# Attention and MLP on one core: quads of four heads on four 64x64 tiles of the array, for batches 2 to 7

## The chip, the cores and the metric

The kernel runs on one core of a Trainium2 chip. The core has a matrix engine (TensorE, PE in the profile; its weight loads are listed apart as PEld), VectorE (DVE), ScalarE (ACT), GpSimd (POOL), which also issues one kind of DMA, and SyncE (SP), which issues the other kind. The engines run their own instruction streams, each in its written order, and wait for one another through semaphores. PE multiplies a stationary operand (loaded into the array as weights, up to 128 rows by 128 columns) with a moving one that streams through, and writes to PSUM: 8 banks, each 128 partitions of 512 fp32 numbers. DVE and ACT read PSUM and write to SBUF. A matmul can use a part of the array: 64 of its rows (a row tile), 64 of its columns (a column tile) or both (64x64). The metric is the device time of a run in microseconds, lower is better.

## The reference

```python
def _attn_ref(q, k, v):                       # (8, 12, 448, 64) each
    scale = 1.0 / np.sqrt(q.shape[-1])
    scores = scale * np.matmul(q, k.transpose(0, 1, 3, 2))
    m = np.max(scores, axis=-1, keepdims=True)
    e = np.exp(scores - m)
    attn = e / (np.sum(e, axis=-1, keepdims=True) + np.exp(-m) + 1e-09)
    return np.matmul(attn, v)

x = attn_out.transpose(0, 2, 1, 3).reshape(B * S, H * D)   # 3584 x 768
h = x @ w_in                                               # 768 x 2048
r = np.maximum(h, 0.0)
out = (r * r) @ w_out                                      # 2048 x 768
```

The softmax has a one added to its denominator. The kernel uses exp(scores) without the maximum, so the denominator is the sum plus 1. Inputs and outputs are fp32, the kernel's operands fp16.

## The kernel before

Attention is worked in units of a batch and a pair of heads; x is kept transposed (`xts`, features on partitions). For one unit the 448 keys are cut into four chunks of 112 (key 4p+t is row p of chunk t). `scores` makes, per chunk, the transposed scores of both heads in PSUM (112 keys on partitions, 2 x 448 queries), and one ACT instruction turns them into exponentials (`exp`, 112x896) in a buffer `et`. In batches 0 to 2 (`ON_PE`) q and k are transposed by PE; there, each head holds 64 partitions. From batch 3 on, a DMA transposes them from a staged fp16 copy in DRAM, which lays even and odd tokens on the two halves of the partitions; so a chunk takes four matmuls of 224 queries, two of them in flight as row tiles of 64 rows. `values` accumulates V times exponentials over the four chunks, the two heads as column tiles (112 rows, 64 columns). `add_chunks` sums the four chunks on DVE; `row_sums` multiplies that by ones (two matmuls), and ACT takes Ln(x + 1) and Exp(-x), the reciprocal `rcp`; `normalise` multiplies values and reciprocal on DVE into `xts`.

The MLP: `tile_in` is a tile of the first product: 128 hidden features by 448 tokens, 6 steps of 2 column tiles (128 rows, 64 columns), then relu and square on DVE (`relu_squared`, two instructions) into a ring `gs`. `tile_out` is a half-tile of the second product: 128 tokens by 384 columns, 16 steps. In the mode `ROWS2` a step is two row tiles (64 rows, 128 columns), which write two banks, `op` and `lo`; DVE reads `op` (L359) and then adds `lo` to it (L363). A batch has 16 tiles of the first product and on the mean 7 half-tiles of the second.

The order of the work is written out by hand (`manual_schedule`). From batch 2 on, the loop takes three units at a time. It goes over their 12 score chunks, and between two chunks it runs 4 or 5 steps of `tile_out` in `ROWS2` (`rows`). Then, in the mode `COLS2`, come the values of the three units before (`take_in`), then `tile_in` tiles with sums between them (`sum_up`). The first product of batch b-1 and the second of b-2 run beside the attention of batch b. After the first three units of a batch, the transposing loads of batch b+1 go to SP's queue; on POOL, `hold` waits for them with a tiny copy, and behind it stand V of b+1 and the staged copy of b+2.

PSUM: scores have two buffers of two banks. Everything else takes one-bank buffers from `mp_tile`, in turn three of `m_psum` and one of `x_psum`: a tile gets its bank once the tile that had it before has been read, and PE waits for that at the new tile's first matmul. A half-tile in `ROWS2` takes two of the four.

Of the kernel before, what the change touches and what calls it, by code (L numbers as in the profile page):

```python
# [8 lines left out]
FP32 = mybir.dt.float32  # L9
# [6 lines left out]
def kernel(  # L16
# [16 lines left out]
    NFFB = DF // 128  # L33
    RUN = 4
    P = S // RUN
    ON_PE = (0, 1, 2)
    COLS = H * S // 2 + 16
    HALF = DM // 2
# [34 lines left out]
    wout_r = moe_w_out.rearrange("(c p) f -> p c f", p=128)  # L73

    whole, vns, qks, xts, naturals, stages = {}, {}, {}, {}, {}, {}

    def load_v(b, p0, p1):
        hs = slice(2 * p0, 2 * p1)
# [62 lines left out]
            )  # L141


    def cast(b, pr):
        for name in "qk":
            f = flat.tile([P, 2, RUN, D], FP16, name=f"flat{name}")
            if pr < 2 and name == "k":
                nc.scalar.activation(out=f, in_=naturals[name, b, pr], func=AF.Copy)
            else:
                nc.vector.tensor_copy(f, naturals[name, b, pr])  # L150
            naturals[name, b, pr] = f
# [26 lines left out]
    def scores(u, et, c, only=(0, 1)):  # L178
        b, pr, q0, n = u
        qk = qks[b]  # L180
        two = [] if n == S else s_psum.tile([P, 2, 512], FP32, name="sp")
        for kk in [2 * c + x for x in only]:
            sp = s_psum.tile([P, 2, 512], FP32, name="sp") if n == S else two
            if b in ON_PE:
                o = 0 if n == S else kk % 2 * n
                for h in range(2):
                    r = slice(64 * h, 64 * h + 64)
                    x = pr * S
                    nc.tensor.matmul(sp[:, h, o:o + n], qk[r, 1, x + P * kk:x + P * kk + P],  # L189
                                     qk[r, 0, x + q0:x + q0 + n], start=True, stop=True)  # L190
            else:
                for h in range(2):
                    for odd in range(2):
                        r = slice(64 * odd, 64 * odd + 64)
                        x = (2 * pr + h) * (S // 2)
                        kx = x + kk // 2
                        which = 1
                        if kk % 2 != odd:
                            which = 2
                            kx += kk % 2  # L200
                        nc.tensor.matmul(sp[:, odd, h * (S // 2):(h + 1) * (S // 2)],  # L201
                                         qk[r, which, kx:kx + 2 * P - 1:2], qk[r, 0, x:x + S // 2],
                                         start=True, stop=True)
            if n == S:
                exp(chunk(et, u, c, kk).rearrange("p (o x) -> p o x", o=2), sp[:, :, 0:S])
        if n < S:
            exp(et[:, 0:RUN * 2 * n].rearrange("p (c h x) -> p c h x", c=2, h=2)[:, c], two[:, :, 0:2 * n])
# [15 lines left out]
    def of_head(e, u, h):  # L223

        b, _, _, n = u
        if n < S:
            return e[:, h]
        if b in ON_PE:
            return e.rearrange("p (h x) -> p h x", h=2)[:, h]
        return e.rearrange("p (o h x) -> p h o x", o=2, h=2)[:, h]  # L230

    def values(u, et, xp, o=0):
        b, pr, _, n = u
# [5 lines left out]
    def row_sums(us, sums):  # L239
# [4 lines left out]
        for j, (u, parts) in enumerate(zip(us, sums)):  # L244
            for x, es in enumerate(parts):
                total = es[:, 0:2 * n]
                if n < S:
                    total = total.rearrange("p (h n) -> p h n", h=2)
                for h in range(2):
                    nc.tensor.matmul(zp[64 * h:64 * h + 64, j * n:(j + 1) * n], ones, of_head(total, u, h),  # L250
                                     start=(x == 0), stop=(x == len(parts) - 1))
        rcp = z_pool.tile([128, 512], FP32, name="rcp")
        nc.scalar.activation(out=rcp[:, 0:m], in_=zp[:, 0:m], func=AF.Ln, bias=one_b)  # L253
# [11 lines left out]
            nc.vector.tensor_mul(xts[b][:, pr:pr + 2, q0:q0 + n], *two)  # L265


    joined = [-1]

    def mp_tile(dtype=FP32):  # L270
# [4 lines left out]

    FULL, COLS2, ROWS2 = range(3)
    mode = [FULL]
    ots = {}  # L280

# [46 lines left out]
    def store(c, ot, n0, n1):  # L328
        end = c + 128
        while c < end:  # L330
            b = c // S
            step = RUN if b in ON_PE else 2
            rows = out[b * S:(b + 1) * S, n0:n1].rearrange("(p t) m -> t p m", t=step)
            t, p = c % S // (S // step), c % S % (S // step)
            m = min(S // step - p, end - c)
            o = c + 128 - end
            nc.sync.dma_start(out=rows[t, p:p + m, :], in_=ot[o:o + m, n0:n1])
            c += m

    def tile_out(tok, n0, w):  # L340
# [1 line left out]
        if n0 == 0:  # L342
            ots[tok] = osb_pool.tile([128, DM], FP32, name="ot")
        ot = ots[tok]
        rows = mode[0] == ROWS2
        op = mp_tile()
        lo = mp_tile() if rows else None
        for fb in range(NFFB):
            g = gs[:, fb, tok % RING:tok % RING + 128]
            if rows:  # L350
                for x, o in ((0, op), (64, lo)):
                    nc.tensor.matmul(o[:, 0:w], g[x:x + 64], wout[x:x + 64, fb, n0:n0 + w],  # L352
                                     start=(fb == 0), stop=(fb == NFFB - 1))
            else:
                product(op[:, 0:w], g, wout[:, fb, n0:n0 + w], start=(fb == 0), stop=(fb == NFFB - 1))
            if fb < NFFB - 1:
# [13 lines left out]

    warm = consts.tile([128, 512], FP16)
    nc.vector.memset(warm, 0.0)
    ones = consts.tile([P, 64], FP16)
    nc.vector.memset(ones, 1.0 / GS)
    one_b = consts.tile([128, 1], FP32)
    nc.vector.memset(one_b, 1.0 / GS)
    for pr in range(3):
# [60 lines left out]

    FIRST = 192
    units = [(0, pr, 0, FIRST) for pr in range(NPAIR)] + [(0, pr, FIRST, S - FIRST) for pr in range(NPAIR)]  # L440
    units += [(b, pr, 0, S) for b in range(1, B) for pr in range(NPAIR)]
    NU = len(units)

    transpose_at = {pr - 1: [(0, pr)] for pr in range(1, NPAIR)}
    for i, at in ((10, (1, 0)), (11, (1, 1)), (11, (1, 2)), (13, (1, 3)), (14, (1, 4)), (15, (1, 5)), (16, (2, 0)),
                  (17, (2, 1))):
        transpose_at.setdefault(i, []).append(at)

    def keep_warm(n):
# [5 lines left out]
    ets, ess, rcps = {}, {}, {}  # L455
    xp = None

    last_of = consts.tile([1, 3, 1], FP16)

    def hold(b):  # L460

        nc.gpsimd.tensor_copy(last_of, qks[b][0:1, :, 0:1])

    def begin(i):
        spare = (i - 3 * NPAIR - 3) % 6
        if i > 3 * NPAIR + 2 and spare in (1, 2):
            ets[i] = nat.tile([P, RUN * 2 * S], FP16, name=f"nn{spare - 1}")
        else:
            ets[i] = e_pool.tile([P, RUN * 2 * S], FP16, name="et")
        es = es_pool.tile([P, 2 * S], FP16, name=f"es{i % 2}")  # L470
        half = es_pool.tile([P, 1024], FP16, name="half")
        ess[i] = (es, half)
# [50 lines left out]
    for i in range(NPAIR, 2 * NPAIR):  # L523
# [28 lines left out]
        if i > NPAIR:  # L552
            drain(share[0] * (0.25 if two else 0.2))
        if i == NPAIR + 5:
            load_natural(2, 0, 3)
            for n0 in (0, HALF):
                for j in range(2):
                    load_wout(n0, j, 2)
# [2 lines left out]
    for i in range(2 * NPAIR, 3 * NPAIR):  # L561
# [6 lines left out]
        scores(u, et, 0)  # L568
        for at in transpose_at.get(i, ()):
            transposes(*at)  # L570
        if i == 2 * NPAIR + 3:
            load_natural(2, 3, 6)
            load_v(2, 0, 6)
            stage(3)
        drain(share[0] * (1.2 if first else 0.45))
        scores(u, et, 1)
# [23 lines left out]

    pending = [3 * NPAIR - 1]
    joined[0] = 0
    complete(S)

    def rows(n):
        mode[0] = ROWS2
        while outs and n > 0:
            one(outs)  # L610
            n -= 1
        mode[0] = COLS2

    def take_in(at):
        xp = mp_tile()
        values(units[at], ets.pop(at), xp)
        normalise([units[at]], xp, rcps.pop(at))

    def add(at, *steps):
        for step in steps:  # L620
            add_chunks(units[at], ets[at], *ess[at], step)

    def sum_up(*ats):
        for at in ats:
            rcps[at] = row_sums([units[at]], (ess.pop(at)[0:1],))

    for i in range(3 * NPAIR, NU, 3):
        b, pr = units[i][0:2]
        for j in range(3):
            begin(i + j)  # L630
            for kk in range(RUN):
                scores(units[i + j], ets[i + j], kk // 2, (kk % 2,))
                if kk == 0 and j:
                    add(i + j - 1, 1, 2)
                if kk == 1:
                    add(i + j, 0)
                if (i, j, kk) == (3 * NPAIR, 0, 2):
                    transposes(2, 2)
                if (j, kk) != (2, RUN - 1):
                    rows(5 if (RUN * j + kk) % 3 == 0 else 4)  # L640
        mode[0] = COLS2
        if i == 3 * NPAIR:
            sum_up(i - 1)
        for at in pending:
            take_in(at)
        if b in ON_PE and pr == 0:
            for x in range(3):
                transposes(b, 3 + x)
        if pr == 0:
            queue((b - 1) * S, S)  # L650
            if b > 2:
                run(outs)
            if b + 1 < B:
                transposed_loads(b + 1)
                hold(b + 1)
                load_v(b + 1, 0, NPAIR)
                if b + 2 < B:
                    stage(b + 2)

        run(ins, 1 if pr == 0 else 2)  # L660
        add(i + 2, 1)
        run(ins, 1)
        add(i + 2, 2)
        sum_up(i, i + 1)
        run(ins, 2)
        sum_up(i + 2)
        run(ins, 3 if pr == 0 else 4)
        if pr:
            complete(b * S)
        pending = [i, i + 1, i + 2]  # L670
    for at in pending:
        take_in(at)
    mode[0] = FULL
    run(outs, 3)
    queue((B - 1) * S, S)
# [31 lines left out]
```

## Time and profile before

| | |
|---|---|
| median of 3 runs | 412.71 us (412.4 to 412.81) |
| span of the profiled execution, its own time | 410.6 us |
| PE busy | 401.9 us (98%) |
| DVE busy | 289.7 us (71%) |
| ACT busy | 234.8 us (57%) |
| POOL busy | 36.1 us (9%) |
| two batches of the steady part, 146 to 239 us | 93.0 us |

The page shows one profiled execution; its 410.6 us lie between the first and the last instruction, the runs' times also hold what lies around that. Matmuls are pipelined: one of 448 columns shows about 0.35 us while the next pair starts 0.19 us later, so the rate is read from the starts, and a busy PE is not PE at its peak. A row of instructions in order of time gives the start, how long they last together, engine, line, operation, out<-in, sizes and count; behind it, in brackets, the engine's idle time before it and who ended that. A row of waits names who waited for whom, the total in us, how often and the longest. A row of busy times has, for a stretch, its length, busy us (and instructions) of PE, PEld, DVE, ACT and POOL, PE's granted clock, the share of the DMA engines and GB/s.

### The profile page before, as it was taken

The page shows a single profiled execution, that of the slowest core. Times are in us where ns is not written, and L with a number is a line of the kernel's source. Part 1 is how long each engine was busy: PE and PEld are TensorE (multiplying, and loading weights), DVE is VectorE, ACT ScalarE, POOL GpSimd, SP SyncE. Part 2 cuts the span into 40 slices and gives each one's busy share as a digit, 9 for nine tenths or more (in the row PEclk, how much of TensorE's full clock was granted, in tenths as well). Part 3 has the DMA queues.
Part 4 walks back from the last instruction along what each step waited for, and adds up shares of the span by engine and source line. Part 5 has one row for each costly group of instructions (what it writes and reads, how often), then busy time and mean ns, then how long its engine had stood idle before and what let it go on. Part 6 is the DMA issues. An engine that isn't in the chain of part 4 may idle for free.

```text
span 410.6 us, 10684 instructions
## 1 busy us (share of the span) xinstructions
PE 401.9 (98%) x4715; PEld 261.0 (64%) x4715; DVE 289.7 (71%) x554; ACT 234.8 (57%) x312; POOL 36.1 (9%) x58
## 2 busy tenths in 40 slices
PE   8899999999999999999999999999999999999997
PEld 3577676865576666666566666667566665555664
DVE  3778889878976787777876788867876789186000
ACT  5899897767393745559383755739464663100111
POOL 7524030020000100001000030001000000000000
PEclk9999999999999999999999999999999999999999
DMA  9999999779114991499304892297102010010222
GB/s 204 197 199 196 203 202 218 134 136 215 54 42 106 137 201 42 96 186 181 102 2 115 167 179 65 78 185 127 41 2 69 11 41 2 38 40 0 78 77 78
DMA packets 75823, 45.58 MB, mean 111 GB/s; under 512 B 42560, under 2 KB 72000, under 8 KB 75456
## 3 DMA queue, kind: packets, MB, share of 16 engines
q0 software_dynamic: 28848, 22.16, 35.6%
q1 hardware_dynamic: 46208, 22.05, 23.7%
q8 instruction: 37, 0.61, 0.6%
q10 hardware_dynamic: 720, 0.69, 0.5%
q14 instruction: 10, 0.08, 0.1%
HBM read 45.69 MB, written 17.93 MB: 155 GB/s over the span
## 4 chain that ended last, share of the span: by engine, by line
PE 91%; DVE 4%; ACT 3%; issue 1%
PE mp L286 26%; PE mp L352 16%; PE mp L288 10%; PE xp L352 7%; PE xp L286 6%; PE sp L201 6%; PE mp L236 5%; PE xp L288 4%; PE xp L236 3%; PE sp L189 3%; ACT et L169 3%; PE mp L250 2%; PE mp L158 1%; PE mp L452 1%; DVE half L218 1%
## 5 line engine op out<-in xcount | busy, mean ns | idle before, releaser
L169 ACT ACTIVATE et<-sp 112x896 f16<-112x896 f32 (+2 forms) x144 | 125.6, 916 | 42.4 <-PE sp L201 30.6
L286 PE MATMUL mp<-xt,win 128*64 128x448 f16 (+2 forms) x1296 | 115.4, 325 | 0.7 <-DVE xt L262 0.6
L352 PE MATMUL mp<-wout,gs 64*128 64x384 f16 x848 | 115.1, 323 | 0.0
L286 PEld LDWEIGHTS <-win 128*64 128x64 f16 x1536 | 85.1, 110 | 44.7 <-issue 1.8
L293 DVE TENSOR_SCALAR rt<-mp 128x448 f16<-128x448 f32 (+2 forms) x104 | 64.7, 622 | 31.1 <-PE mp L286 18.5
L352 PEld LDWEIGHTS <-gs 64*128 64x128 f16 x1152 | 58.0, 94 | 21.3 <-issue 0.2
L352 PE MATMUL xp<-wout,gs 64*128 64x384 f16 x304 | 62.4, 323 | 0.0
L295 DVE TENSOR_TENSOR gs<-rt 128x448 f16<-128x448 f16 (+2 forms) x128 | 50.2, 392 | 4.4
L201 PE MATMUL sp<-qk 64*112 64x224 f16 x480 | 43.1, 258 | 0.0
L169 ACT ACTIVATE nn<-sp 112x896 f16<-112x896 f32 x48 | 41.7, 917 | 1.6
L253 ACT ACTIVATE rcp<-mp,one_b 128x448 f32<-128x448 f32 (+2 forms) x35 | 22.1, 633 | 32.2 <-PE mp L250 32.2
L361 ACT ACTIVATE ot<-mp 128x384 f32<-128x384 f32 (+2 forms) x16 | 7.5, 471 | 57.5 <-PE mp L288 41.2
L201 PEld LDWEIGHTS <-qk 64*112 64x112 f16 x480 | 30.6, 128 | 14.3 <-issue 3.6
L288 PEld LDWEIGHTS <-gs 128*128 128x128 f16 x256 | 24.4, 98 | 15.1 <-issue 0.4
L236 PEld LDWEIGHTS <-vn 112*64 112x64 f16 x432 | 22.5, 109 | 15.1 <-issue 3.2
L288 PE MATMUL mp<-wout,gs 128*128 128x384 f16 (+2 forms) x192 | 29.5, 313 | 0.0
L214 DVE TENSOR_TENSOR es<-et 112x896 f16<-112x896 f16 x30 | 18.7, 623 | 14.0 <-ACT et L169 13.6
L254 ACT ACTIVATE rcp<-rcp 128x448 f32<-128x448 f32 (+2 forms) x48 | 27.7, 577 | 1.5
L189 PE MATMUL sp<-qk 64*112 64x448 f16 (+2 forms) x192 | 26.1, 320 | 1.0 <-ACT et L169 0.4
L216 DVE TENSOR_TENSOR es<-es,half 112x896 f16<-112x896 f16 x42 | 26.2, 623 | 1.0
L286 PE MATMUL xp<-xt,win 128*64 128x448 f16 x240 | 26.1, 352 | 0.0
L262 DVE TENSOR_TENSOR xt<-mp,rcp 128x448 f16<-128x448 f32 x29 | 18.0, 621 | 2.9 <-ACT rcp L254 1.1
(63 smaller groups left out, 345.2 us busy)
## 6 DMA issues: line engine op xcount, KB each, us to landing
vn<-in_v_dram POOLq DMA_DIRECT2D x7, 672.0 KB, 8.8
out_dram<-ot SPq DMA_DIRECT2D x9, 384.0 KB, 2.3
win<-in_moe_w_in_dram POOLq DMA_DIRECT2D x8, 384.0 KB, 14.2
wout<-in_moe_w_out_dram POOLq DMA_DIRECT2D x4, 768.0 KB, 18.0
stage_q<-in_q_dram POOLq DMA_DIRECT2D x4, 676.0 KB, 11.6
stage_k<-in_k_dram POOLq DMA_DIRECT2D x4, 676.0 KB, 14.9
out_dram<-ot SPq DMA_DIRECT2D x8, 288.0 KB, 8.7
out_dram<-ot SPq DMA_DIRECT2D x9, 192.0 KB, 2.7
```

The source lines that it names most:

```text
L169: nc.scalar.activation(out=out_, in_=in_, func=AF.Exp, scale=scale)
L189: nc.tensor.matmul(sp[:, h, o:o + n], qk[r, 1, x + P * kk:x + P * kk + P], qk[r, 0, x + q0:x + q0 + n], start=True, stop=True)
L201: nc.tensor.matmul(sp[:, odd, h * (S // 2):(h + 1) * (S // 2)], qk[r, which, kx:kx + 2 * P - 1:2], qk[r, 0, x:x + S // 2], start=True, sto ...
L216: nc.vector.tensor_add(es, es, half[:, 0:2 * S])
L236: nc.tensor.matmul(xp[64 * h:64 * h + 64, o:o + n], vns[b][:, 2 * pr + h, kk, :], of_head(chunk(et, u, kk // 2, kk), u, h), start=(kk == 0 ...
L253: nc.scalar.activation(out=rcp[:, 0:m], in_=zp[:, 0:m], func=AF.Ln, bias=one_b)
L254: nc.scalar.activation(out=rcp[:, 0:m], in_=rcp[:, 0:m], func=AF.Exp, scale=-1.0)
L286: nc.tensor.matmul(out_[x:x + 64], lhsT[:, x:x + 64], rhs, start=start, stop=stop)
L288: nc.tensor.matmul(out_, lhsT, rhs, start=start, stop=stop)
L293: nc.vector.tensor_scalar(out=rt[:, 0:m], in0=hp[:, 0:m], scalar1=0.0, scalar2=None, op0=ALU.max)
L295: nc.vector.tensor_mul(gs[:, f0:f0 + per, t0 % RING:t0 % RING + n], r, r)
L352: nc.tensor.matmul(o[:, 0:w], g[x:x + 64], wout[x:x + 64, fb, n0:n0 + w], start=(fb == 0), stop=(fb == NFFB - 1))
```

## The change

In batches 2 to 7 a unit is now a quad: two pairs of heads, 4g to 4g+3 or, from batch 3 on, two of each half of the heads. The keys are cut into 7 chunks of 64. Each step on PE is four matmuls of 64 rows and 64 columns, on the four quarters of the array:

- `visit`: the scores of one chunk of a quad (64 keys of two heads on the two halves of the partitions, 2 x 448 queries), and one exponential of 128x896.
- `values_quad`: V times exponentials; row half i and column half j are the four heads; the results take two banks.
- `add_quad`: the 7 chunks summed on DVE: 1792 wide (two chunks with two), 1792, 896 and 896.
- `sums_quad`: the sums of four heads in two banks; for a batch's third quad as column tiles with `half_ones`. Ln and Exp twice on ACT, 448 wide each.
- `tile_out`: the mode `ROWS2` becomes `SQUARE`: each step's two matmuls are cut into two by columns.

A batch has three quads m, m+1, m+2. The new loop has two groups per batch, made by `between`: 11 visits with three half-tiles of the second product, then 10 visits with four. Between two visits `between` runs pieces of values or sums that are named by visit number, and steps of `tile_out` up to a share of time. Behind each group come 8 tiles of the first product, in `COLS2`. On POOL `tail_keys` (four copies of 64x384 that gather the last 64 keys) takes the place of `hold`; V comes in two or four loads a batch, q and k of batch 2 in loads of 64 partitions; batch 2's output rows are stored with a step of 7. Batches 0 and 1 and the last stage stay as they were.

```diff
+    QUADS = [(b, g) for b in range(2, B) for g in range(NQ)]
+    def visit(m, c):
+        b, g = QUADS[m]
...
+        sp = s_psum.tile([128, 2, 512], FP32, name="sp")
...
+                        h = H // 2 * i + 2 * g + j
+                        if c == KC - 1:
+                            keys = kms[b][r, h, :]
...
+                            keys = qk[r, which, x:x + 190:3]
+                        nc.tensor.matmul(sp[64 * i:64 * i + 64, o, j * n:(j + 1) * n], keys,
+                                         qk[r, 0, h * n:(h + 1) * n], start=True, stop=True)
+        exp(chunk_quad(m, c).rearrange("p (o x) -> p o x", o=2), sp[:, :, 0:S])
...
+    def sums_quad(m, in_cols):
+        es = esq.pop(m)[:, 0:2 * S]
+        zqs[m] = []
+        for i in range(2):
+            zp = mp_tile()
...
+                    r = slice(64 * i, 64 * i + 64)
+                    nc.tensor.matmul(zp[64 * j:64 * j + 64, 0:S], ones[r], of_column(es[r], m, j),
+                                     start=True, stop=True)
+            zqs[m].append(zp)
+        for i in range(2):
+            rcp = z_pool.tile([128, 512], FP32, name="rcp")
+            nc.scalar.activation(out=rcp[:, 0:S], in_=zqs[m][i][:, 0:S], func=AF.Ln, bias=one_b)
+            nc.scalar.activation(out=rcp[:, 0:S], in_=rcp[:, 0:S], func=AF.Exp, scale=-1.0)
+            zqs[m][i] = rcp
+    def values_quad(m):
+        b, g = QUADS[m]
+        xps = [mp_tile(), mp_tile()]
+        for c in range(KC):
+            e = chunk_quad(m, c)
+            for i in range(2):
+                for j in range(2):
+                    r = slice(64 * i, 64 * i + 64)
+                    nc.tensor.matmul(xps[i][64 * j:64 * j + 64, 0:S], vns[b][r, g, j, c, :], of_column(e[r], m, j),
+                                     start=(c == 0), stop=(c == KC - 1))
+            if c == KC - 1:
...
+                for i in range(2):
+                    nc.vector.tensor_mul(xts[b][:, NQ * i + g, :], xps[i][:, 0:S], zqs[m][i][:, 0:S])
...
+            yield
@@ tile_out @@
-                for x, o in ((0, op), (64, lo)):
-                    nc.tensor.matmul(o[:, 0:w], g[x:x + 64], wout[x:x + 64, fb, n0:n0 + w],
-                                     start=(fb == 0), stop=(fb == NFFB - 1))
+                for y in (0, 64):
+                    for x, o in ((0, op), (64, lo)):
+                        nc.tensor.matmul(o[y:y + 64, 0:w], g[x:x + 64, y:y + 64], wout[x:x + 64, fb, n0:n0 + w],
+                                         start=(fb == 0), stop=(fb == NFFB - 1))
@@ the loop @@
+    STEP = HALF / 2.4
+    PIECE = S / 2.4
+    def second(ns):
+        mode[0] = SQUARE
+        while outs and ns > STEP / 2:
+            ns -= one(outs)
+        return ns
+    def between(visits, tiles, ns, extras):
+        tiles = min(tiles, len(outs))
+        kept = outs[tiles:]
+        del outs[tiles:]
+        ns += tiles * NFFB * STEP
+        spent = 0.0
+        late = []
+        for n, (m, c) in enumerate(visits):
+            visit(m, c)
+            for at in late:
+                add_quad(*at)
+            late = {3: [(m, 0)], 5: [(m, 1), (m, 2)], 6: [(m, 3)]}.get(c, [])
+            spent += PIECE
+            for f in extras.get(n, ()):
+                spent += f() or 0.0
+            spent += max(0.0, (n + 1) * ns / len(visits) - spent) - second((n + 1) * ns / len(visits) - spent)
+        second(1e9)
+        outs[:] = kept
+        return late
...
+    for b in range(2, B):
+        m = NQ * (b - 2)
+        extras = {10: [summed(m)]}
+        ns = 12 * PIECE
+        if b > 2:
+            gen = values_quad(m - 1)
+            for n, w in ((1, 3), (2, 4)):
+                extras[n] = [pieces(gen, w)]
+            ns += KC * PIECE
+        between([(m, c) for c in range(KC)] + [(m + 1, c) for c in range(4)], 3, ns, extras)
         mode[0] = COLS2
...
+        queue((b - 1) * S, S)
+        if b + 1 < B:
+            transposed_loads(b + 1)
+            tail_keys(b + 1)
+            load_v_quads(b + 1)
+            if b + 2 < B:
+                stage(b + 2)
+        run(ins, 2)
+        add_quad(m + 1, 0)
+        run(ins, 6)
+        gen, gen1 = values_quad(m), values_quad(m + 1)
+        extras = {6: [summed(m + 1)]}
+        for n, w in ((0, 3), (1, 4)):
+            extras[n] = [pieces(gen, w)]
+        extras[8] = [pieces(gen1, 3)]
+        extras[9] = [pieces(gen1, 4)]
+        between([(m + 1, c) for c in range(4, KC)] + [(m + 2, c) for c in range(KC)],
+                4, (11 + 2 * KC) * PIECE, extras)
         mode[0] = COLS2
...
+        run(ins, 1)
+        add_quad(m + 2, 3)
+        run(ins, 1)
+        sums_quad(m + 2, True)
+        run(ins, 6)
+        complete(b * S)
```

## The prediction

> **What bounds the kernel now.** I read the page first, then busy times over two batches of the steady part (146 to 239 us), then PE's waits, then the instructions in order of time.
>
> ```profile
> span 410.6 us, 10684 instructions
> PE 401.9 (98%) x4715; PEld 261.0 (64%) x4715; DVE 289.7 (71%) x554; ACT 234.8 (57%) x312; POOL 36.1 (9%) x58
> PEclk9999999999999999999999999999999999999999
> 146.00:192.50 46.50, 46.50 (x568) 30.19 (x566) 35.73 (x68) 27.83 (x37) 2.14 (x4) 1.00 0.74 137
> 192.50:239.00 46.50, 46.50 (x566) 30.00 (x564) 35.73 (x68) 27.89 (x37) 3.29 (x7) 1.00 0.48 104
> PE mp L286 <- DVE xt L262: 0.6, 1, 0.6
> ```
>
> PE has work in flight all the time, at full clock, and a batch takes 46.5 us. A busy PE alone proves little, so I add the batch up from starts of instructions:
>
> ```profile
> 179.50 2.44 PE L286 MATMUL mp<-xt,win 128*64 128x448 f16 x24
> 181.77 1.30 PE L286 MATMUL xp<-xt,win 128*64 128x448 f16 x12
> ...
> 183.00 0.40 PE L201 MATMUL sp<-qk 64*112 64x224 f16 x4
> 183.44 0.92 ACT L169 ACTIVATE et<-sp 112x896 f16<-112x896 f32 x1 [2.50 <-PE sp L201]
> ...
> 189.43 0.35 PE L201 MATMUL sp<-qk 64*112 64x224 f16 x4
> 189.62 0.32 PE L352 MATMUL mp<-wout,gs 64*128 64x384 f16 x1
> 189.62 0.32 PE L352 MATMUL xp<-wout,gs 64*128 64x384 f16 x1
> 189.78 0.65 PE L352 MATMUL mp<-wout,gs 64*128 64x384 f16 x6
> 189.98 0.56 DVE L359 TENSOR_SCALAR ot<-mp 128x384 f32<-128x384 f32 x1 [0.42 <-PE xp L352]
> ...
> 190.64 0.56 DVE L363 SCALAR_TENSOR_TENSOR ot<-xp,ot 128x384 f32<-128x384 f32 x1
> ```
>
> 24 matmuls of 448 columns in column pairs start over 2.27 us: 0.189 us a pair. A pair of 384 columns takes 0.162 (189.62 to 189.78), a score chunk 0.192 (189.43 to 189.62). A batch has 24 score chunks (4.61 us), 24 value pairs (4.54), 6 pairs of sums (1.13), 96 pairs of the first MLP product (18.12) and 112 of the second (18.2): 46.6 against 46.5 measured. So PE streams without a hole, and both columns and holes count in full.
>
> **What the change removes.** Per batch 24 score chunks become 21 groups of four matmuls (-0.58 us), 24 value pairs 21 groups (-0.57), 6 pairs of sums 2 groups and 2 pairs (-0.38): -1.52 us, over six batches -9.1. The second product is cut into twice as many instructions, the same columns. The transposes of batch 2 go from 96 to 84: at 0.98 us for 32 (a row at 32.81 us) -0.4. Together **-9.5 us**, if four 64x64 matmuls start together as two do now. The trace has no 64x64 tile. Lower bound: 0.162 and 0.189 per group, since even a single 128x128 matmul of 384 columns takes 0.162 (48 in 7.8 us). Upper bound: every group costs two pairs, +159 us (112 x 0.162 + 44 x 0.189, six times). I take the lower end, nearest to the pairs, which start in the same instant whether they split rows or columns.
>
> A rule speaks against it. Weight loads last 94 ns for 64x128, 110 for 128x64, and are hidden. The Trainium skill, "TensorEngine Tiling (Array Packing)", Restrictions, says that column tiling switches off fast weight loading, and "TensorE: Matmul & The Clock Gate", LDWEIGHTS, gives columns/1.2 ns, 53 ns for 64. Were the four loads of a group to follow one another at that, a group would take 213 ns: by this estimate 6.7 us more per batch, 40 in all. The trace has two such loads in 0.189 us beside full streaming, which doesn't exclude it for four.
>
> **What it adds: waits for PSUM.** In the program before, four one-bank buffers go round, and nothing but second-product half-tiles (two banks each) runs between score chunks, so a half-tile has a whole other half-tile to be read out. Now `between` starts values and sums, two banks each, in the middle of half-tiles; the next one gets the banks just finished. What each matmul waits for stands in the built program. Call the front group's half-tiles A, B, C, the back group's D to G.
>
> Prices: last matmul to TENSOR_SCALAR 0.36 (189.62 to 189.98); from there to the adding read 0.66, which lasts 0.56; DVE's end to PE 0.04 (the chain has 79.99 to 80.03). Score to exponential 0.44, exponential 0.92, Ln 0.63, Exp 0.58. Last value matmul to product with `rcp` 0.40, the product 0.62. An addition takes 0.62 at 896; at 1792 I estimate 1.08, from 0.39 at 448 and 0.62 at 896.
>
> 1. B waits for A's two reads (batches 3, 5, 7; in 4 and 6 for the first only; not in 2). From A's last group: floor 0.36+0.66+0.56+0.04 = 1.62, less 0.16 of streaming, 1.46. But DVE holds ahead of them two products with `rcp` and the first 1792-wide addition, which needs the fourth exponential; this ends near 0.75, so reads start there: 0.75+0.66+0.56+0.04-0.16 = **1.85**, or 1.2.
> 2. The first tile of the first MLP product after the front group takes a bank of the sums, so it waits for their Ln. That stands on ACT behind the last visit's exponential: 0.44+0.92+0.63+0.04 = 2.03 after the visit, where PE arrives at 0.19+0.19+4x0.162 = 1.03: **1.0**.
> 3. G waits for F: both reads in 3, 5, 7, with one visit between: 1.62-0.16-0.19 = **1.27**; the first read in 4, 6: **0.6**.
> 4. After the back group the first MLP tile waits for the product with `rcp` of the values that ended 0.7 us before. On DVE that stands behind an addition that needs the ninth visit's exponential, and ACT is late. From the start of the visit that has the sums: its exponential ends at 1.33 (exponentials in a row come every 0.89), Ln and Exp twice to 3.75, the next two exponentials to 5.55; the 1792 and the 896 addition to 7.3, the product to 7.9. PE: 0.19+0.19+7x0.162 = 1.52 for this visit; 0.19, wait 3 and 8 groups to 3.62; 0.19+3x0.19+5x0.162 to 5.19; 0.19+4x0.19+3x0.162 to 6.63. So **1.3**; after the longer wait 3 PE is 0.67 later: **0.67**.
> 5. The second MLP tile waits for G's second read in 3, 5, 7: two products and two reads last from 7.3 to 9.7, the first MLP tile (1.13) ends at 9.1: **0.67** with the 0.04.
> 6. Then the column sums wait for the last addition, which stands behind the first tile's relu (0.65+0.31) and lasts 0.62: to 11.2, where PE is at 10.2: **1.1**, or **0.42** after wait 5.
>
> Batches 3, 5, 7: 1.85+1.0+1.27+0.67+0.67+0.42 = 5.9; batches 4, 6: 1.2+1.0+0.6+1.3+1.1 = 5.2. Batch 2 has no wait 1; its Ln wait 2 is 1.1, before the leftover sums of batch 1, whose chain to the first tile grows by 0.3; its last half-tile takes the bank of sums made 0.54 before, free at 2.0 (1.5); and waits 4 to 6 are as in 4 and 6 (2.4): 5.3. Sum **33.3 us**. Bounds: with floors alone (no addition or exponential ahead) about 4.3, 3.0 and 3, 22 in all; with each a quarter longer, 41.
>
> The Trainium skill's "TensorEngine Tiling (Array Packing)", PSUM Bottleneck, warns that tiling speeds TensorE but not the reading of PSUM; here DVE's 0.56 us reads are unchanged, and no rate of theirs is exceeded. By that rule alone nothing is added; the cost is that PE arrives too early.
>
> **Edits I cost at nothing.** V in four issues a batch instead of one, 0.95 us each on POOL, which is 9% busy; landing took 8.8 us, needed a batch later. `tail_keys` (four copies, where one of three elements stood): between 0.2 us, that row, and 0.62 each, DVE's copy of 896; used 25 us later; if they held DVE at a critical place, +2. Queued behind them on POOL are V and the stage copies, all due a batch later. On SP the transposing loads gain only an old wait. Batch 2's loads put 0.46 MB ahead of `wout`: at 200 GB/s 2.3 us, and `wout` landed about 61, used at 66.5: 0, at most +2. PE mode switches stay four a batch. ACT loses 18 of 144 exponentials, off the path except in waits 2 and 4.
>
> **Sum.** 410.6 - 9.5 + 33.3 = 434.4 us of span. The median stands 2.1 us above the span (412.7 to 410.6): **436 us**, 5.7% slower.
>
> **Rivals.** (a) *The waits are mostly covered, the saved columns win.* 1.6 us a batch break even (9.5/6). This needs waits 2 to 6 covered by the time that wait 1 gives ACT and DVE to catch up; then 412.7-9.5+3x1.85+2x1.2 = 411, and with wait 1 gone 403. For it: DVE idles 23% and ACT 40% of a batch. Against: the waits are order, not load; PE can't pass a waiting matmul, and floors alone are 22 us. 7%. (b) *Four tiles don't stream at once,* or loads or instruction fetch (eight instructions per 0.162 us, now four) limit a group. From about +20 ns a group it would show as +19 us, 455; fully serial 595. Against: pairs start together and loads overlap in both splits. 8%. (c) *Floors only*: 425. It lies in the main case, which has 85%.
>
> **Range.** Floors: 412.7-9.5+22 = 425. High: waits a quarter longer (+8), 2.5 ns more per group (936 groups, +2.3), `wout` and POOL (+4): 450. I stretch the low end to 422. Faster by over 0.2% (about what this kernel's measurement can tell from no change): 0.05, and within: 0.02, both from (a); slower: 0.93.
>
> **What would show it.** Right: PE's waits name the reads of the second product, the Ln and the product with `rcp`, some 5 to 6 us a batch; a batch takes about 50.5 us; groups still start 0.162 and 0.189 apart. Wrong: groups further apart with few waits (b), or a batch under 46.5 us (a).

## The result, and the profile after

| | before | after |
|---|---|---|
| median | 412.59 us (412.40 to 412.81, 4 runs) | 436.19 us (433.92 to 442.51, 4 runs) |
| ratio, 95% interval | | 1.0553 [1.0512, 1.0595] |
| profiled execution: time, span | 410.6 us span | 433.92 us, 432.1 us span |

The changed kernel is 5.5% slower; 436 had been predicted. (One of the four runs, 442.51, and one of the last experiment's six, 411.74, had a granted clock of 0.992; the ratios leave them out, and without them the two medians are 434.56 and 405.17.)

The page of the profile after, and its busy times in the same two stretches of 46.5 us (length, PE, PEld, DVE, ACT, POOL with instructions, PE's granted clock, DMA share, GB/s):

```profile
span 432.1 us, 14530 instructions
PE 400.1 (93%) x6627; PEld 286.3 (66%) x6627; DVE 289.7 (67%) x531; ACT 218.7 (51%) x289; POOL 60.6 (14%) x93
PEclk9999999999999999999999999999999999999999
146.00:192.50 46.50, 43.19 (x808) 32.84 (x804) 34.08 (x61) 23.75 (x31) 5.16 (x9) 1.00 0.57 113
192.50:239.00 46.50, 42.77 (x850) 32.00 (x842) 32.75 (x57) 24.83 (x32) 6.16 (x10) 1.00 0.57 115
```

PE now idles 3.3 and 3.7 us per stretch, at full clock; DVE and ACT are no busier than before. So no engine has become the bound: PE waits for engines that have time. For what, PE's waits in the profile after say (engine, tile and line of the waiting matmul, whom it waited for, total us, times, longest):

```profile
PE xp L489 <- DVE ot L500: 6.7, 6, 1.5
PE mp L422 <- DVE xt L399: 4.0, 6, 1.0
PE mp L422 <- ACT rcp L380: 3.5, 5, 0.7
PE mp L371 <- DVE half L361: 2.6, 6, 0.7
PE mp L489 <- DVE ot L496: 1.6, 2, 0.8
PE mp L422 <- DVE qk L192: 1.3, 1, 1.3
...
PE xp L422 <- DVE ot L500: 1.0, 3, 0.3
```

These are the reads of the second product (L496 and L500: waits 1 and 3, and 5 at L422), the Ln (L380: wait 2), the product with `rcp` (L399: wait 4) and the last addition (L361: wait 6). The sixth row had not been predicted. Places in the order of time, in batch 3 and, in the last line, batch 4:

```profile
122.35 0.32 PE L489 MATMUL mp<-wout,gs 64*64 64x384 f16 x1
124.14 0.32 PE L489 MATMUL xp<-wout,gs 64*64 64x384 f16 x1 [1.47 <-DVE ot L500]
...
157.96 1.33 PE L422 MATMUL mp<-xt,win 128*64 128x448 f16 x12 [0.51 <-DVE xt L399]
159.62 1.32 PE L422 MATMUL xp<-xt,win 128*64 128x448 f16 x12 [0.33 <-DVE ot L500]
161.11 0.57 PE L371 MATMUL mp<-half,half_ones 128*64 128x448 f16 x4 [0.17 <-DVE half L361]
...
174.47 0.52 PE L489 MATMUL mp<-wout,gs 64*64 64x384 f16 x7 [0.81 <-DVE ot L496]
```

The bracket understates a loss, because the profile draws a matmul of 384 columns 0.32 us long while the next group could start after 0.163. From start to start, 122.35 to 124.14, wait 1 loses 1.79 - 0.16 = 1.63 us. All losses below are taken so. The groups of four stand 0.19 us apart at 448 columns (169.66, 169.85) and 0.163 at 384 (150.49, 150.65, 150.81).

A batch is counted from one score chunk to the same chunk of the next batch. Before, from the first chunk of a batch's second three units, at 183.00 (shown with the prediction) and

```profile
230.18 0.40 PE L201 MATMUL sp<-qk 64*112 64x224 f16 x4
277.36 0.40 PE L201 MATMUL sp<-qk 64*112 64x224 f16 x4
```

that is 47.18 us. After, from the first chunk of a front group:

```profile
117.43 0.40 PE L345 MATMUL sp<-qk 64*64 64x224 f16 x8
168.42 0.40 PE L345 MATMUL sp<-qk 64*64 64x224 f16 x8
218.32 0.40 PE L345 MATMUL sp<-qk 64*64 64x224 f16 x8
```

51.0 us for an odd batch, 49.9 for an even one, and the same again in batches 5 and 6 (269.31, 319.21). Of the 21.5 us between the two spans, 5.4 lie before the front group of batch 3 (its first chunk starts at 117.43 us, against 112.06), 13.1 in batches 3 to 6 (201.8 us against 188.7), and 3.0 after that.

### The profile page after: what moved, and what is told of

The parts are those of the page before. It is cut to its first block, busy times and chain, and to the rows that moved or that the text cites. A ratio compares the mean times of both kernels' runs of the same rounds, so it can differ in the third digit from the quotient of the medians.

```text
span 432.1 us, 14530 instructions
## 1 busy us (share of the span) xinstructions
PE 400.1 (93%) x6627; PEld 286.3 (66%) x6627; DVE 289.7 (67%) x531; ACT 218.7 (51%) x289; POOL 60.6 (14%) x93
## 4 chain that ended last, share of the span: by engine, by line
PE 73%; DVE 14%; ACT 7%; issue 4%; DMA 1%; DVEq 0%; ACTq 0%
PE mp L422 19%; PE mp L489 16%; PE mp L424 10%; PE xp L422 6%; PE sp L345 4%; PE xp L489 4%; PE mp L393 4%; PE xp L424 3%; DVE xt L399 2%; ACT et L221 2%; ACT nn L221 2%; ACT rcp L380 2%; PE sp L240 2%; DVE ot L496 2%; DVE ot L500 2%
## 5 line engine op out<-in xcount | busy, mean ns | idle before, releaser
L221 ACT ACTIVATE et<-sp 128x896 f16<-128x896 f32 (+3 forms) x132 | 118.2, 916 | 102.6 <-PE sp L345 82.0
L489 PE MATMUL mp<-wout,gs 64*64 64x384 f16 x1952 | 134.7, 323 | 3.1 <-DVE ot L496 1.6
L422 PEld LDWEIGHTS <-win 128*64 128x64 f16 x1536 | 96.2, 110 | 46.1 <-issue 15.8
L422 PE MATMUL mp<-xt,win 128*64 128x448 f16 (+2 forms) x1248 | 110.4, 324 | 9.5 <-DVE xt L399 4.0
L489 PEld LDWEIGHTS <-gs 64*64 64x64 f16 x2624 | 90.9, 107 | 31.1 <-issue 14.6
L489 PE MATMUL xp<-wout,gs 64*64 64x384 f16 x672 | 67.7, 323 | 6.7 <-DVE ot L500 6.7
L221 ACT ACTIVATE nn<-sp 128x896 f16<-128x896 f32 x42 | 38.1, 914 | 17.8 <-PE sp L345 16.1
L345 PE MATMUL sp<-qk 64*64 64x224 f16 x720 | 37.7, 258 | 0.0
L496 DVE TENSOR_SCALAR ot<-mp 128x384 f32<-128x384 f32 x41 | 22.6, 552 | 20.4 <-PE mp L489 11.4
L345 PEld LDWEIGHTS <-qk 64*64 64x64 f16 x720 | 27.9, 119 | 7.5 <-issue 3.6
L422 PE MATMUL xp<-xt,win 128*64 128x448 f16 x288 | 31.8, 353 | 1.0 <-DVE ot L500 1.0
L399 DVE TENSOR_TENSOR xt<-mp,rcp 128x448 f16<-128x448 f32 x29 | 17.0, 619 | 21.1 <-PE mp L393 13.4
L380 ACT ACTIVATE rcp<-mp,one_b 128x448 f32<-128x448 f32 x26 | 16.3, 626 | 27.0 <-PE mp L371 27.0
L393 PE MATMUL mp<-et,vn 64*64 64x448 f16 x266 | 21.7, 349 | 0.0
L381 ACT ACTIVATE rcp<-rcp 128x448 f32<-128x448 f32 x36 | 20.8, 577 | 1.1
```

The source lines that it names most:

```text
L221: nc.scalar.activation(out=out_, in_=in_, func=AF.Exp, scale=scale)
L345: nc.tensor.matmul(sp[64 * i:64 * i + 64, o, j * n:(j + 1) * n], keys, qk[r, 0, h * n:(h + 1) * n], start=True, stop=True)
L380: nc.scalar.activation(out=rcp[:, 0:S], in_=zqs[m][i][:, 0:S], func=AF.Ln, bias=one_b)
L381: nc.scalar.activation(out=rcp[:, 0:S], in_=rcp[:, 0:S], func=AF.Exp, scale=-1.0)
L393: nc.tensor.matmul(xps[i][64 * j:64 * j + 64, 0:S], vns[b][r, g, j, c, :], of_column(e[r], m, j), start=(c == 0), stop=(c == KC - 1))
L399: nc.vector.tensor_mul(xts[b][:, NQ * i + g, :], xps[i][:, 0:S], zqs[m][i][:, 0:S])
```

## The experiments

Two questions. Is the loss the order of half-tiles, values and sums on four banks (the prediction), or do 64x64 tiles cost something themselves (rival b)? And are the columns saved where nothing waits?

**One wait undone: the values first.** In the front group the values of a quad are no longer put into a half-tile; all seven stand right after the first score chunk.

```diff
-            for n, w in ((1, 3), (2, 4)):
-                extras[n] = [pieces(gen, w)]
+            extras[0] = [pieces(gen, KC)]
```

> The changed kernel with one edit: in the front group the seven value groups of the batch before all come right after the first visit, ahead of half-tile A, so no half-tile is begun with only values between it and the one whose banks it takes. Theory 1 (the time goes into waits for PSUM banks, which the order makes): PE's wait for the reads of half-tile A, 1.6 us in batches 3, 5, 7 and 1.0 us in 4 and 6, goes and nothing comes in its place: 3 x 1.6 + 2 x 1.0 = 6.8 us less, a span of 425 us against 432. Theory 2 (four 64x64 matmuls or their weight loads stream more slowly, the order is innocent): unchanged, 432.

Measured 428.68 us (427.88 to 429.67), ratio 1.0392 [1.0373, 1.0412], span 427.9. Wait 1 is gone from the front group, and the Ln wait behind that group too: its last half-tile now has eight groups left after the sums instead of four, so PE comes 0.65 us later. What came instead is 0.34 us on an exponential. Batch 3 takes 48.97 us (51.0 in the changed kernel), batch 4 48.75 (49.9). The third took 52.5 in this execution, 3.5 us longer than its like, for the stops described at the end. The other three executions have spans of 426.0 to 427.0: some 6 us less than the changed kernel's 432.1, where 6.8 was expected.

**One wait undone: the sums later.** The sums of the front group come as column tiles behind the second tile of the first MLP product.

```diff
-        extras = {10: [summed(m)]}
-        ns = 12 * PIECE
+        extras = {}
+        ns = 11 * PIECE
...
+        sums_quad(m, True)
```

> The changed kernel with one thing undone: in the front group the four-tile row sums no longer stand after the last visit; they come as column tiles after the second tile of the first MLP product. All else is as it was, waits 1 and 3 to 6 too. Theory of the prediction (wait 2 is PE arriving at a bank of the sums before their Ln, which is late behind the last visit's exponential): the first MLP tile then takes a bank that was read long before, and the sums take the banks of the last half-tile, read while two tiles run. The loss at that place, 0.86 us in the trace of the changed kernel, falls to the 0.09 of the tile-shape change in batches 3 to 7, and the 0.93 of batch 2 goes too; sums as column tiles cost 0.19 more in each of six batches: 5 x 0.77 + 0.93 - 6 x 0.19 = 3.6 us less, median about 432.5, span about 428.5, and the wait of the first MLP tile for rcp (3.5 us in five) gone. Rival (the Ln only happened to be the last of several that end together; the half-tile's reads are late next): the wait changes its name, and the time stays at 436 or gains under 1 us.

Measured 433.71 us (431.65 to 433.96), ratio 1.0506 [1.0489, 1.0523], span 429.8 (432.1 in the changed kernel): 2.3 us less in the span, and in the median 0.9 less than the 434.56 above, where 3.6 was expected. In the time the expectation is not met; place by place it holds: in all of batches 3 to 7 the loss behind the front group fell from 0.86 to 0.09, and the row of the first tile's wait for L380 left PE's waits. In batch 2 1.55 us went. With 6 x 0.19 for the sums as column tiles that is 5 x 0.77 + 1.55 - 1.14 = 4.3 less, and this execution also started 0.7 earlier; 2.6 came back through one gap in batch 3. So the wait was what the theory said, and did not just change its name; that such a gap took back the gain in the other executions too is not shown (last section).

**The second product alone.** The kernel before, with nothing changed but each step of the second product cut into four 64x64 matmuls.

```diff
-                for x, o in ((0, op), (64, lo)):
-                    nc.tensor.matmul(o[:, 0:w], g[x:x + 64], wout[x:x + 64, fb, n0:n0 + w],
-                                     start=(fb == 0), stop=(fb == NFFB - 1))
+                for y in (0, 64):
+                    for x, o in ((0, op), (64, lo)):
+                        nc.tensor.matmul(o[y:y + 64, 0:w], g[x:x + 64, y:y + 64], wout[x:x + 64, fb, n0:n0 + w],
+                                         start=(fb == 0), stop=(fb == NFFB - 1))
```

> The kernel before with one part of the change alone: a step of the second product is four 64x64 matmuls instead of two of 64x128; pairs of heads, 112 keys and the whole order stay. Theory 1: a group of four starts every 0.162 us as a pair does, so 412.6 us if going between 64x128 and 64x64 tiles is free; if each such change costs the 0.09 us that the trace shows between column pairs and row pairs, 24 x 2 x 0.09 = 4.3 us a batch, 26 in all: 439. Theory 2: at least 20 ns more per group, 96 groups a batch, 12 us or more, and groups of the second product that start further apart than 0.18 us.

Measured 447.2 us (447.13 to 447.27), ratio 1.0841 [1.0823, 1.0859], span 445.2. That is more than any theory gave it. PE by lines in the kernel before and in this one (busy us, mean ns, idle before), then this one in the order of time:

```profile
L201 PE MATMUL sp<-qk 64*112 64x224 f16 x480 | 43.1, 258 | 0.0
L201 PEld LDWEIGHTS <-qk 64*112 64x112 f16 x480 | 30.6, 128 | 14.3 <-issue 3.6
```

```profile
L201 PE MATMUL sp<-qk 64*112 64x224 f16 x480 | 48.3, 280 | 0.0
L201 PEld LDWEIGHTS <-qk 64*112 64x112 f16 x480 | 21.9, 127 | 37.1 <-issue 37.1
```

```profile
197.28 0.40 PE L201 MATMUL sp<-qk 64*112 64x224 f16 x4
197.61 1.01 PE L353 MATMUL mp<-wout,gs 64*64 64x384 f16 x20
198.54 0.40 PE L201 MATMUL sp<-qk 64*112 64x224 f16 x4
198.88 0.84 PE L353 MATMUL mp<-wout,gs 64*64 64x384 f16 x16
199.65 0.40 PE L201 MATMUL sp<-qk 64*112 64x224 f16 x4
```

Inside the second product nothing is lost: 20 matmuls are five groups, 0.81 us. But from the score chunk (64x112) to the second product (64x64) it now takes 0.33 us, where it took 0.19 in the program before, and from the last group to the next chunk 0.12 more (198.54 - 197.61 = 0.93, against 0.81). So a chunk between 64x64 tiles costs 0.14 + 0.12 = 0.26 us at this place; over the 144 chunks of six batches the 34.6 us of span make 0.24 each. The weight loads before the chunks, idle for "issue" 3.6 us before and 37.1 now, are where the profile puts it. No step of the prediction had this, since in the changed kernel all of a group's tiles are 64x64. PE is busy 436.5 us here, 98%, as in the kernel before: the busy share hides this loss completely.

**All but the second product.** The changed kernel with that edit undone alone (steps of two 64x128 matmuls, mode `SQUARE` otherwise).

> The changed kernel with one part undone: a step of the second product is two row tiles of 64x128 again; everything else, the order and the banks above all, stays. Theory 1: the same waits at the same places, 4.9 us a batch in 3, 5, 7 and 3.9 in 4 and 6: 432 us of span if changes between 64x128 and 64x64 are free, up to 26 us more if each costs 0.09. Theory 2: faster by 20 ns x 112 x 6 = 13 us or more, about 419.

Measured 455.09 us (454.51 to 455.78), ratio 1.1032 [1.1016, 1.1048], span 453.4. The same six waits are there (the reads of the second product 5.6 us in six, the Ln 3.0 in five, the additions 2.6 in six), and a change of tile shape at both sides of every visit comes on top: 21.3 us over 126 visits are 0.17 each, net of the waits that it shortened. Here too a chunk and the next step start 0.34 us apart (236.97 and 237.31) where 0.19 is the rate. Rival (b), that the second product's four tiles or their loads cost the time, would have made this kernel 13 us or more faster than the changed one. It is some 20 us slower. Since the change of shape costs time as well, this run alone doesn't exclude (b); the starts do: in the changed kernel and with the second product alone, groups of four stand 0.163 us apart.

**The order alone.** The same quads and the same 64x64 tiles, in another order: a half-tile, or a quad's values, is finished before the next thing takes banks; one quad's values go to the back group and the other two to the next front group; all sums come as column tiles between tiles of the first MLP product, long after their last addition. The reciprocals of a quad share one fp16 tile.

```diff
-    def between(visits, tiles, ns, extras):
+    def between(visits, works):
...
+            while gens and spent + STEP / 2 < (n + 1) * ns / len(visits):
+                got = next(gens[0], None)
+                if got is None:
+                    gens.pop(0)
+                else:
+                    spent += got
...
-        between([(m, c) for c in range(KC)] + [(m + 1, c) for c in range(4)], 3, ns, extras)
+        between([(m, c) for c in range(KC)] + [(m + 1, c) for c in range(4)],
+                ([held(m - 2), held(m - 1)] if b > 2 else []) + half_tiles(3))
...
+        between([(m + 1, c) for c in range(4, KC)] + [(m + 2, c) for c in range(KC)], [held(m)] + half_tiles(4))
+        mode[0] = COLS2
+        run(ins, 1)
+        add_quad(m + 2, 3)
+        run(ins, 1)
+        sums_quad(m + 1, True)
+        run(ins, 2)
+        sums_quad(m + 2, True)
```

> The changed kernel's quads and 64x64 tiles in another order: a half-tile or a set of values is finished before the next takes its banks; values of quads m+1 and m+2 come first in the next batch's front group, those of m first in the back group; all sums stand as column tiles between tiles of the first product, two tiles behind the addition that they need; the reciprocals of a quad are fp16, in one buffer. Theory 1: the six kinds of waits go. Per batch 47.2 us before, less 1.5 for the columns saved, plus 0.4 for sums as column pairs: 46.1, so about 1.1 x 6 = 6.6 us less than before, and 1.5 more for the wait at batch 2's transposes, which stays: 407.5 us. Theory 2: the streaming stays slow, 428 us or more.

Measured 406.7 us (406.05 to 407.85), ratio 0.9861 [0.9842, 0.9881], span 405.0: 1.4% faster than the kernel before. The page's PE row, the busy times of the two stretches, and PE's longest waits:

```profile
PE 394.9 (98%) x6627; PEld 262.0 (65%) x6627; DVE 292.2 (72%) x531; ACT 221.0 (55%) x289; POOL 58.6 (14%) x93
```

```profile
146.00:192.50 46.50, 46.50 (x924) 31.48 (x912) 37.48 (x66) 26.68 (x34) 6.14 (x10) 1.00 0.69 131
192.50:239.00 46.50, 46.50 (x916) 31.23 (x910) 37.74 (x65) 26.22 (x34) 8.71 (x14) 1.00 0.65 128
```

```profile
PE xp L272 <- DVE xt L301: 1.3, 2, 1.0
PE mp L423 <- DVE qk L192: 1.3, 1, 1.3
PE mp L592 <- DVE warm L510: 1.2, 1, 1.2
PE mp L423 <- issue: 0.7, 1, 0.7
```

None of the six waits is left (the first and third of these rows lie in the start, the second in batch 1, and the fourth is a gap of batch 5, described at the end). The instructions are as many as in the changed kernel, 6627 on PE, in the same shapes but for the sums. Front groups start at 156.57 and 202.59: 46.02 us a batch, against 47.18 before; batch 5, with that gap, takes 47.25. The fp16 reciprocals are no rival: the product with `rcp` lasts 0.62 us in this kernel as in the changed one.

**And the wait that was not predicted.** The order above, and in the last unit of batch 1 the key transposes of a quad come only after the unit's MLP tiles.

```diff
-            transposes_quad(2, i - 2 * NPAIR - 4)
+            transposes_quad(2, i - 2 * NPAIR - 4, (0, 1) if i < 3 * NPAIR - 1 else (0,))
...
         if i == 3 * NPAIR - 1:
+            transposes_quad(2, 1, (1,))
```

> The reordered quads (406.7 us) with one more change: batch 1's last unit does the query transposes of the second quad before its MLP tiles as before, and the key transposes only after them. There an MLP tile lost 1.47 us to the two copies of these transposes, which stand on DVE behind four other instructions. Theory (the wait is a bank that is held by the copy, not a lack of DVE time): with one bank held the tiles go on, the second copy is late for nobody, and 1.3 to 1.5 us go: 405.3. Rival (DVE itself is behind at this place, so the tiles wait for their own relu instead): the wait gets another name, and under 0.5 us goes: 406.3 or more.

Measured 405.66 us (404.76 to 411.74, 6 runs), ratio 0.9841 [0.9823, 0.9858], span 403.1. The tile's loss of 1.47 us is gone, but 0.71 more came at the sums that follow, which the profile names "PE mp L286 <- DVE qk L192": both theories are half right. A bank was held, and DVE was behind too. 0.8 us of the span is the split; the other 1.1 is two gaps of batch 5 (0.83 and 0.33) that the trace of the order before had, and this one hasn't. The ratios of the two can't be told apart. Its median is the lowest of the study.

## Why the prediction was right, step by step

The time came out right (436.19 for 436), and so did the places of the six waits and what PE waits for there. That the number is so close is partly luck: the waits were 6.4 us smaller than predicted, and 4.1 us came from outside the sum.

**The base of a batch: wrong by 0.7 us.** The prediction took the stretch from 146 to 239 us for two batches and found 46.6 us from the pieces, "so PE streams without a hole". The stretch was chosen by eye, here and in the table of the time before. From repeat to repeat a batch takes 47.18. The pieces left out 0.09 us at each of four changes of tile shape (the chunk at 183.00 starts 0.29 us after the last pair of the first product, where pairs stand 0.19 apart); with these they make 46.96, and 0.22 lies in gaps too small to name. The total did not suffer, as it was added to the span. But the forecast of 50.5 us a batch was met (51.0 and 49.9) with a base too low and waits too long.

**The columns, -1.52 us a batch: right.** The order alone shows it. It keeps the sums as six pairs, so it should save 1.52 - 0.38 = 1.14; 47.18 - 46.02 = 1.16. Four 64x64 tiles start together every 0.163 and 0.19 us, the lower of the two bounds. By the loads estimated from the Trainium skill, "TensorE: Matmul & The Clock Gate", LDWEIGHTS, with "TensorEngine Tiling (Array Packing)", Restrictions, a group would have taken 213 ns: here a 64x64 load shows 107 ns (106 in the second product alone), longer than the 53 of the page's formula, and four of them still hide in a group of 163 ns.

**The six waits, 33.3 us: the places right, the sizes too large.** Losses from start to start (without the 0.09 of a shape change), against the prediction:

| | odd batches | predicted | even batches | predicted |
|---|---|---|---|---|
| 1, second half-tile of the front group | 1.63 | 1.85 | 0.97 | 1.2 |
| 2, first MLP tile, Ln | 0.77 | 1.0 | 0.77 | 1.0 |
| 3, last half-tile | 1.12 | 1.27 | 0.46 | 0.6 |
| 4, first MLP tile, product with `rcp` | 0.58 | 0.67 | 0.81 | 1.3 |
| 5, second MLP tile | 0.49 | 0.67 | none | none |
| 6, column sums | 0.33 | 0.42 | 0.85 | 1.1 |
| sum | 4.9 | 5.9 | 3.9 | 5.2 |

Batch 2 loses 5.0 us at these places and its own, of which the kernel before already lost 0.6: 4.4, for 5.3 predicted. In all 3 x 4.9 + 2 x 3.9 + 4.4 = 26.9 us, between the floors (22) and the estimate. At the two places worked out here, what is missing lies in what stands ahead on DVE and ACT, and hardly in PE's arrival; the other places are not worked out. For wait 1, DVE after the values, in the changed kernel:

```profile
120.78 1.16 DVE L399 TENSOR_TENSOR xt<-mp,rcp 128x448 f16<-128x448 f32 x2 [2.19 <-PE mp L393]
121.87 1.09 DVE L355 TENSOR_TENSOR half<-et 128x1792 f16<-128x1792 f16 x1
122.88 0.55 DVE L496 TENSOR_SCALAR ot<-mp 128x384 f32<-128x384 f32 x1
123.53 0.56 DVE L500 SCALAR_TENSOR_TENSOR ot<-xp,ot 128x384 f32<-128x384 f32 x1
```

The 1792-wide addition took 1.09 (1.08 was estimated), the reads 0.65 apart and 0.56 long as the prediction had them. But the first read starts 0.53 us after the last group of A (122.35), not 0.75: 0.53 + 0.65 + 0.56 + 0.05 - 0.16 = 1.63. For wait 4 in batch 4 the products end 7.5 us after the visit that has the sums, not 7.9, while PE is there after 6.7 us (6.63 predicted).

**What the prediction did not have.** Batch 1's last unit: an MLP tile waits for the two copies of `transposes_quad`, 1.47 us from start to start; the program before loses 0.80 nearby. The transposes had been costed by their columns alone (-0.4), with no word on who holds the bank. The copies on POOL took 0.80 us each, above the upper bound of 0.62, and nothing waited for them: right for its reason (needed 25 us later), wrong in its bound. And about 0.4 us a batch is left between 47.18 - 1.52 + the waits (50.6 and 49.5) and the periods measured, in gaps too small to show among the waits; the order alone has no such rest.

**So the sum** 410.6 - 9.5 + 33.3 was met by 410.6 - 9.5 + 26.9 = 428.0 and 4.1 us outside its terms: the rest of 0.4 in five batches, 0.7 more in batch 1, 0.7 of a later start, which one profiled execution has and another has not, and 0.7 that I can't break down. The waits were put 6.4 us too high, and what made up for most of that was put at nothing: that the two nearly cancel is luck.

**The rivals.** (a), 403 to 411, does not happen to this kernel, but a kernel without the waits was run, and its 405.66 lies in that range. That the waits are "order, not load" is shown by the order alone: with the same matmuls on PE but for the sums, and DVE at 72%, they vanish. (b) fell with the starts of the groups, in the changed kernel and with the second product alone. (c), floors alone, would be 425: the waits, 26.9 us, ended between its 22 and the 33.3 of the likeliest case.

## What to carry to other kernels

When a faster arrangement makes PE reach a tile sooner, look at which bank that tile takes and which instruction has to read it first: on four banks in turn, a two-bank result put into the middle of another made PE lose 1.6 us to two reads of 0.56 us each, with DVE busy 67% of the span. Before giving up such a change, order the work so that each result is read while another, already begun, streams; here that turned +5.5% into -1.4%. Keep tiles of one shape together, and count a period from one instruction to its repeat, not from a stretch that looks right.

## What the runs showed of the hardware

**Tiles of another shape between tiles.** A score chunk of 64x112 between second-product steps of 64x64 costs 0.24 us, in both changes together, which the steps of 64x128 did not (0.19 to the next step there). Between tiles of 112 and of 128 columns the change was free; to 64 columns it wasn't.

**Gaps without a wait for data, and the clock after a stop.** Three of the kernels with quads (the values first, the sums later, the order alone) have, at one place of the profiled execution, a gap that the profile puts down to "issue". From start to start it loses 0.7, 2.2 and 0.8 us. In the kernel with the sums later, in the order of time and then by stretches:

```profile
154.04 0.32 PE L489 MATMUL xp<-wout,gs 64*64 64x384 f16 x1
156.43 0.32 PE L489 MATMUL mp<-wout,gs 64*64 64x384 f16 x1 [2.06 <-issue]
```

```profile
153.00:156.40 3.40, 1.37 (x33) 0.95 (x26) 2.52 (x4) 0.92 (x1) 0.00 (x0) 1.00 1.11 230
156.43:157.84 1.41, 1.41 (x16) 0.73 (x17) 0.79 (x2) 0.00 (x0) 0.00 (x0) 1.00 0.49 125
157.90:161.20 3.30, 3.30 (x21) 1.87 (x19) 2.31 (x5) 0.12 (x1) 0.00 (x0) 0.50 0.21 74
161.30:165.00 3.70, 3.70 (x42) 2.70 (x40) 2.60 (x7) 2.09 (x4) 0.00 (x0) 1.00 0.01 2
```

In the middle of a half-tile PE starts nothing for 2.4 us. For 1.4 us after that its granted clock is still 1.00, then 0.50 for 3.3 us, and 1.00 again; at 0.50, pairs of 448 columns start 0.375 us apart, half as often as before. All four executions of this kernel have a mean granted clock of 0.995 or 0.996, so each may have had such a stop.

In the kernel with the values first a stop of 2.0 us is followed by the same: 1.00 from 257.6 to 259.0 us, then 0.50 to 262.4. But that stop, which begins 2.3 us after the gap of 0.7, has a wait that the profile names: PE waits for a read of the second product, and DVE stands idle before its reads for the store of an earlier `ot`.

```profile
256.35 0.56 DVE L496 TENSOR_SCALAR ot<-mp 128x384 f32<-128x384 f32 x1 [1.42 <-DMA out_dram<-ot]
257.62 1.32 PE L422 MATMUL xp<-xt,win 128*64 128x448 f16 x12 [1.85 <-DVE ot L500]
```

DVE waits as long for a store beside the gap of the order alone (1.4 us, to 240.37); the 0.33 us lost after that gap is PE waiting for DVE (L430). Why these stores land late is open. In the changed kernel the longest loss in this part is 1.63 us, and the clock of its profiled execution never falls. In these traces, then, a stop of 2 us or more was followed by half the clock, and one of 1.6 was not.

For the gap itself there is a trace of a cause, not more. The queue that carries instructions moved 37 packets (0.61 MB) in the kernel before and 52 (0.85 MB) in these three. One of its packets falls into the gap, while the DMA engines are full (from 154.0 to 155.2 us):

```profile
q0 software_dynamic: 18, 0.28, 118.6%
...
q8 instruction: 1, 0.02, 4.8%
```

That PE had run out of instructions is argued from this, not shown: the changed kernel moved 52 packets too, without such a gap in its profile, and no run took instructions or transfers away. It would be the next thing to try, since the stops add 1.2 to 3.5 us to the three executions here, and may be why the quads' runs scatter over 1.3 to 3.9 us where those of the program before stay within 1.
